# A planner's order searched anew, with later landings of weights and of two batches: packed attention and a squared-ReLU layer on one core

## The chip, the core and the metric

The kernel runs on one core of a Trainium2 chip. The metric is the device time of one execution in microseconds (us). Five engines work in parallel, each through its own queue and in the order in which the program puts instructions into it: TensorE (PE; PEld are its weight loads), VectorE (DVE), ScalarE (ACT), GpSimd (POOL) and SyncE (SP). POOL, SP and ACT also issue the transfers between the device memory and the core's memory. An engine whose first instruction waits holds all that stand behind it.

## What is computed

Eight batches of eight heads, 576 positions, 64 channels a head, and 32 packing queries p per head and batch:

```python
def sm_attn(qq, kk, vv):
    a = softmax(scale * qq @ kk.T)        # per batch and head
    return a @ vv
p_packed = sm_attn(p, k, v)               # 32 x 64 per head
x = sm_attn(q, p_packed, p_packed)        # 576 x 64 per head
h = x.reshape(4608, 512) @ w_in           # 512 x 2048
out = (relu(h) ** 2) @ w_out              # 2048 x 512
```

The second attention has only 32 keys. The kernel never forms x: it multiplies p_packed by w_in first (a matrix M per batch) and the softmax rows by M.

## The kernel before

The work is cut into 1,329 pieces, each with a name, one or two engines that can run it, a cost in us, and the pieces that it needs. For batch b they are:

- `Lk`, `Lv`, `Lq`: loads of k, v and q, issued on POOL, which also converts to bf16 on the way. `LWI.c.i.qd` are the quarters of the four column chunks c of w_in, `LWO.c` the eight chunks of w_out. Each load is two pieces, the issue and the transfer.
- `Tk`, `Tq` (lines 700 and 697 on DVE, 706 on SP for batches 5 to 7): k and q transposed.
- `S1` (PE, line 733 or 749), `MX` (row maximum, DVE, 752), `EX` (exponential, ACT, 760), `E`/`EC` (its transposition, PE 766 and a copy; for batches 5 to 7 `E` is a transposing transfer on SP, line 772), `PV` (PE, 780), `XN`, `XM`, `XC` (normalize, transpose, copy out): the packing attention.
- `M.b.c` (PE, 810): M for chunk c of w_in, copied out by `MC` (ACT line 606 or DVE line 608).
- `S2` (PE, 827 or 837), then the softmax over 32 keys: `SI` (848), `SM` (854), `SU` (858) on DVE, `SE` (exponential, ACT, 861), `SS` (864, 865), `SN` (871), `SO` (875) on DVE. Batch 0 does this in three parts of 128, 192 and 256 positions, named `.0.0`, `.0.1` and `.0.2`.
- `F` (batches 0 and 1, PE line 912) or `F1` (the others, line 884): softmax rows times M into an accumulator pair; `R` (ReLU, ACT 920/894 or DVE 922/896); `Q` or `SQ` (square, ACT 930/902 or DVE 932/904) into the tile gT.
- `F2.t` (PE, 938): 128 rows of the output, sixteen products each, copied out by `FC`. For six groups of four row tiles `GP` (PE, 1005; seven products in two halves of eight instructions) with sums `GS` and `GC` (DVE, 990 and 1025) stand instead. `FZ` (956) is one tile in two halves. `ST` are the stores (line 950).

A planner (`Plan.forward`, from line 73) places these pieces in time when the program is built. It steps through time, and at each moment an engine takes, among the pieces that are ready by the planner's own costs, the one that is lowest in level plus the piece's number in `TABLE['o']`; `TABLE['l']` leans a piece toward DVE or ACT. Only the order of each engine's queue, and the engine, go into the program; on the chip the queues then run as data and buffers allow. A transfer is a piece of a "DMA" engine that runs them one after another; its data counts as there when the piece ends, plus `lag`:

```python
def load(name, us, fn, issue, deps=()):
    old = [issued[-8]] if len(issued) >= 8 else []
    add(f"{name}i", [("POOL", issue, fn)], list(deps) + old, line="load", lag=2.0, level=-200)
    add(name, [("DMA", us, None)], [f"{name}i"], line="dma", lag=0.9, level=-200)
```

Two more rules matter. Where PE changes between kinds of pieces (`mode`: whole-array products 0, `S1` and `S2` 1, `PV` 2, `M` and the later `S1`/`S2` 3) the planner charges `TURN` = 0.111 us. And where PE would idle for 0.7 us or more before the first `F2`, `fills` (line 205) puts products of a zero tile into its queue (line 612), so that PE stays busy; they are in the program for good, and a piece behind them waits for them even when its data is there.

The queues of SP (transposing transfers and stores), ACT (copies, exponentials, ReLU) and DVE are in the planner's hands in the same way; loads are issued by POOL in a fixed list.

Of the kernel before, what the change touches and what calls it, by code (L numbers as in the profile page):

```python
# [14 lines left out]
P = 128  # L15
# [26 lines left out]
class Plan:  # L42
# [185 lines left out]
TABLE = {'o': {'Lk.0.0i': -41.988702, 'Lk.0.1i': 172.502158, 'Lk.0.0': 181.505648, 'LP.0': -6.041854, 'Lk.0.1':  # L228
# [289 lines left out]
def kernel_impl(tc, q, k, v, p, w_in, w_out, out):  # L518
# [23 lines left out]
    with ExitStack() as ctx:  # L542
# [485 lines left out]
        add = plan.add  # L1028
# [36 lines left out]
        for x in ORDER.split():  # L1065
# [29 lines left out]
            elif x[0] == "a":  # L1095
                for i in range(2):
                    for qd in QDS:
                        load(f"LWI.{n}.{i}.{qd}", 0.7 + 0.45 * ((n, i, qd) in ((1, 0, 0), (3, 0, 0), (3, 1, 1))), lambda n=n, i=i, qd=qd: dma_w_in(n, i, qd), 0.6)
# [297 lines left out]
```

## Time and profile before

| | |
|---|---|
| median of 3 runs | 235.95 us (235.69 to 235.96) |
| the profiled execution's own time | 235.75 us |
| its span, first to last instruction | 234.0 us |
| PE / DVE / ACT / POOL busy | 221.4 / 198.1 / 152.0 / 59.9 us |
| PE instructions of line 612 (zero products) | 97, 14.6 us |
| moved by DMA | 34.06 MB |

In a row of a timeline the first two numbers are start and length in us, then follow engine, line, operation, operands and count; in brackets stands the idle time before it and what ended it. A row of the chain of waits has start, length and what the end was waiting for. In a table of stretches each engine's busy time stands in the order of the heading. A row of waits has the total, the number and the longest.

### The profile page before, as it was taken

The numbers are of one execution on the slowest core, as the hardware profiler recorded it, in microseconds if no ns is written. First come the engines' busy times: TensorE is split into PE (matmuls) and PEld (weight loads), VectorE is DVE, ScalarE is ACT, GpSimd is POOL, SyncE is SP. The second block draws the span as 40 slices with busy tenths as digits, with TensorE's granted clock in tenths as the row PEclk, the third lists the DMA queues.
The fourth block names the chain that finished last, engine by engine and source line by source line (L and its number), as shares of the span: only waits on it lengthen the run. The fifth ranks groups of instructions, "written<-read, shape, count | busy, mean of one in ns | idle before, by whom it ended". The sixth has DMA issues, their size and how long they took to land.

```text
span 234.0 us, 6384 instructions
## 1 busy us (share of the span) xinstructions
PE 221.4 (95%) x2621; PEld 159.9 (68%) x2638; DVE 198.1 (85%) x332; ACT 152.0 (65%) x247; POOL 59.9 (26%) x107
## 2 busy tenths in 40 slices
PE   8878899999999999999999999999999999999991
PEld 5655665346554566678768787877777888888781
DVE  3769887799999988999999789999999999877240
ACT  3333897469875799984999846459985998501100
POOL 9777745233343666620000000000000000000000
PEclk9999999999999999999999999999999999999998
DMA  7999999999999999999788689609710023205316
GB/s 235 179 169 175 195 204 204 204 194 250 240 205 241 227 220 177 174 182 125 175 150 135 134 116 191 140 2 204 134 39 8 4 44 73 65 0 112 70 43 181
DMA packets 46716, 34.06 MB, mean 146 GB/s; under 512 B 25376, under 2 KB 38432, under 8 KB 46688
## 3 DMA queue, kind: packets, MB, share of 16 engines
q0 software_dynamic: 19456, 18.03, 48.8%
q1 hardware_dynamic: 26304, 14.98, 29.8%
q10 hardware_dynamic: 928, 0.66, 0.9%
q8 instruction: 20, 0.33, 0.6%
q14 instruction: 8, 0.07, 0.1%
HBM read 37.22 MB, written 9.44 MB: 199 GB/s over the span
## 4 chain that ended last, share of the span: by engine, by line
PE 77%; DMA 14%; DVE 3%; POOL 1%; issue 1%; SPq 1%; ACT 0%; DVEq 0%; POOLq 0%
PE ps L1005 29%; PE ps L884 20%; PE ps L938 13%; DMA kq_b<-in_q_dram 7%; PE ps L912 5%; PE ps L810 3%; DMA w_in_b<-in_moe_w_in_dram 3%; DMA v_b<-in_v_dram 3%; DMA out_dram<-o_sb 2%; PE ps L956 1%; PE ps L780 1%; PE ps L827 1%; SPq L950 1%; PE ps L733 1%; POOL v_b L621 1%
## 5 line engine op out<-in xcount | busy, mean ns | idle before, releaser
L894 ACT ACTIVATE r_b<-ps 128x576 bf16<-128x576 f32 x92 | 52.8, 662 | 8.5 <-PE ps L884 8.3
L884 PE MATMUL ps<-a,M 128*128 128x288 bf16 x384 | 52.5, 286 | 0.2
L884 PEld LDWEIGHTS <-M 128*128 128x128 bf16 x384 | 37.3, 98 | 11.6 <-DVE a L875 0.2
L938 PE MATMUL ps<-w_out_b,gT 128*128 128x512 bf16 x159 | 41.2, 380 | 1.3 <-issue 0.6
L1005 PEld LDWEIGHTS <-gT 128*128 128x128 bf16 x384 | 36.9, 98 | 7.5 <-issue 2.4
L606 ACT CAST M<-ps 128x1024 bf16<-128x1024 f32 (+1 forms) x33 | 29.8, 940 | 10.9 <-PE ps L810 8.7
L904 DVE TENSOR_TENSOR gT<-r_b 128x1152 bf16<-128x1152 bf16 x40 | 29.3, 745 | 4.0 <-ACT r_b L894 3.7
L606 ACT COPY o_sb<-ps 128x512 f32<-128x512 f32 (+1 forms) x21 | 11.9, 575 | 30.5 <-PE ps L1005 16.6
L950 POOL DMA_DIRECT2D out_dram<-o_sb x2 | 1.1, 570 | 119.2 <-DVE o_sb L1025 117.7
L1005 PEld LDWEIGHTS <-gS 128*128 128x128 bf16 x288 | 27.7, 98 | 5.1 <-issue 1.8
L938 PEld LDWEIGHTS <-gT 128*128 128x128 bf16 x176 | 15.8, 98 | 15.3 <-issue 2.5
L1025 DVE TENSOR_TENSOR o_sb<-o_sb,ps 128x512 f32<-128x512 f32 x30 | 20.3, 676 | 6.5 <-PE ps L1005 5.7
L1005 PE MATMUL ps<-wS,gT 128*128 128x256 bf16 x192 | 23.5, 273 | 0.5 <-DVE o_sb L1025 0.5
L1005 PE MATMUL ps<-w_out_b,gT 128*128 128x256 bf16 x192 | 23.8, 273 | 0.0
L1005 PE MATMUL ps<-wS,gS 128*128 128x256 bf16 x192 | 23.5, 273 | 0.0
L920 ACT ACTIVATE r_b<-ps 128x512 bf16<-128x512 f32 (+2 forms) x25 | 15.7, 664 | 7.7 <-PE ps L912 6.4
L912 PE MATMUL ps<-a,M 128*128 128x256 bf16 (+3 forms) x160 | 18.6, 262 | 1.3 <-DVE M L608 0.8
L912 PEld LDWEIGHTS <-M 128*128 128x128 bf16 x160 | 13.8, 98 | 6.4 <-issue 1.1
L760 ACT ACTIVATE e<-ps,n 128x576 bf16<-128x576 f32 x16 | 11.7, 737 | 7.0 <-DVE n L752 6.8
L612 PE MATMUL ps<-o_sb 128*128 128x256 bf16 x97 | 14.6, 311 | 1.1 <-DVE o_sb L615 1.1
L752 DVE TENSOR_REDUCE n<-ps 128x1 f32<-128x576 f32 x16 | 11.6, 750 | 2.0 <-PE ps L733 1.8
L612 PEld LDWEIGHTS <-o_sb 128*128 128x128 bf16 x97 | 10.2, 111 | 4.4 <-DVE o_sb L615 1.1
(77 smaller groups left out, 316.9 us busy)
## 6 DMA issues: line engine op xcount, KB each, us to landing
out_dram<-o_sb SPq DMA_DIRECT2D x65, 128.0 KB, 3.4
kq_b<-in_k_dram POOLq DMA_DIRECT2D x14, 288.0 KB, 10.9
kq_b<-in_q_dram POOLq DMA_DIRECT2D x10, 288.0 KB, 6.9
w_in_b<-in_moe_w_in_dram POOLq DMA_DIRECT2D x16, 128.0 KB, 6.1
w_out_b<-in_moe_w_out_dram POOLq DMA_DIRECT2D x8, 256.0 KB, 9.4
v_b<-in_v_dram POOLq DMA_DIRECT2D x5, 320.0 KB, 11.4
v_b<-in_v_dram POOLq DMA_DIRECT2D x12, 128.0 KB, 7.7
v_b<-in_v_dram POOLq DMA_DIRECT2D x5, 256.0 KB, 9.8
```

The source lines that it names most:

```text
L606: nc.scalar.copy(dst, src)
L612: nc.tensor.matmul(half(7)[:, :2 * P], lhsT=zero[:, :P], rhs=zero, start=True, stop=True)
L752: nc.vector.tensor_reduce(n1[b % 2][:, qd:qd + 1], ps1[b, qd], axis=AX.XY if b in XBAR else AX.X, op=ALU.max, negate=True)
L760: nc.scalar.activation(e_out(qd) if b in XBAR else e1[:, qd, :S], ps1[b, qd], ACT.Exp, bias=n1[b % 2][:, qd:qd + 1], accum_out=d1[b % 2][: ...
L884: nc.tensor.matmul(t[:, c], lhsT=M[b % 2][:, qd, fb * FB:(fb + 1) * FB], rhs=a2[b % 2][:, qd, c * HALF:(c + 1) * HALF], start=(qd == 0), s ...
L894: nc.scalar.activation(dst, src, ACT.Relu)
L904: eng.tensor_tensor(out=dst, in0=r, in1=r, op=ALU.mult)
L912: nc.tensor.matmul(t[:, c, m * w:(m + 1) * w], lhsT=M[b % 2][:, qd, fb * FB:(fb + 1) * FB], rhs=a2[b % 2][:, qd, o:o + w], start=(qd == 0) ...
L920: nc.scalar.activation(dst, ph["h", b, x, j], ACT.Relu)
L938: nc.tensor.matmul(po[t], lhsT=gT[:, fb, n0:n0 + P], rhs=w_out_b[:, fb, :], start=(fb == 0), stop=(fb == NFB - 1))
L1005: nc.tensor.matmul(pz[g, k][:, i], lhsT=a[:, f, i * P:(i + 1) * P], rhs=w[:, f], start=(k not in ON and h == 0 and f == 0 and i == 0), sto ...
L1025: nc.vector.tensor_tensor(out=oC(g, i, j), in0=oC(g, *src), in1=pz[g, z], op=ALU.add)
```

## The change

All numbers of `TABLE` are new. Besides, two lines of the planner's input change:

```diff
-            add(name, [("DMA", us, None)], [f"{name}i"], line="dma", lag=0.9, level=-200)
+            late = 0.8 * (name[:3] == "LWO" or name.split(".")[:2] in (["LWI", "1"], ["LWI", "2"], ["LWI", "3"]) or name[:2] != "LW" and name.split(".")[1] in "12")
+            add(name, [("DMA", us, None)], [f"{name}i"], line="dma", lag=0.9 + late, level=-200)
...
-                        load(f"LWI.{n}.{i}.{qd}", 0.7 + 0.45 * ((n, i, qd) in ((1, 0, 0), (3, 0, 0), (3, 1, 1))), lambda n=n, i=i, qd=qd: dma_w_in(n, i, qd), 0.6)
+                        load(f"LWI.{n}.{i}.{qd}", 0.7 + 0.45 * ((n, i, qd) in ((1, 0, 0), (3, 0, 0))), lambda n=n, i=i, qd=qd: dma_w_in(n, i, qd), 0.6)
...
-TABLE = {'o': {'Lk.0.0i': -41.988702, 'Lk.0.1i': 172.502158, 'Lk.0.0': 181.505648, 'LP.0': -6.041854, 'Lk.0.1':
+TABLE = {'o': {'Lk.0.0i': -36.900503, 'Lk.0.1i': 0.41924, 'Lk.0.0': -16.56608, 'LP.0': 169.009326, 'Lk.0.1':
```

So the planner counts the last three chunks of w_in, all of w_out, and k, v and q of batches 1 and 2 as landing 0.8 us later. No instruction's shape or size changes; what changes is the order. In the two programs, read queue by queue:

- **PE.** Ahead of the last product of `M.0.2` (third chunk of w_in, batch 0) both orders hold the same pieces in the same sequence. Behind it, up to `S1.1`, stood 9 zero products, `F.0.1.0` to `.2`, `M.0.3`, `F.0.2.0` to `.3`, `F.0.1.3`, `F.0.0.2`, `F2.2.0`; now stand `F.0.1.0` to `.2`, `F.0.0.2`, `M.0.3`, `F.0.2.0` to `.5`, 3 zero products, `F.0.2.6`, `F2.3.0`. Zero products are 89 instead of 97. PE changes its kind 65 times behind `M.0.2` instead of 70. In the middle the pieces are dealt anew: between `S1.6` and `PV.6` stand seven halves of `GP`, the four `M.5`, `S2.5` and `XM.5`, where fourteen halves of `GP`, `PV.5` and `S1.7` stood besides the same `M.5`, `S2.5` and `XM.5`; `S1.3` and `S1.4` come earlier. From `GP.1.6` to the end PE's order is the same.
- **ACT and DVE.** Around `M.0.2` ACT had `R.0.0.1`, `MC.0.2.0`, `SE.0.2`, `MC.0.2.1`, `R.0.1.0` to `.2`, `MC.0.3.1`, `R.0.2.0`, `R.0.2.1`; it now has `SE.0.2`, `R.0.0.1`, `Q.0.0.1`, `MC.0.2.1`, `R.0.1.0` to `.2`, `R.0.0.2`, `MC.0.3.1`, `R.0.2.0` to `.2`, `Q.0.2.2`, `R.0.2.3`. `MC.0.2.0` goes to DVE, behind `SS.0.2`; both halves of `MC.0.1` go to ACT. Some 70 pieces in all change their engine.
- **POOL** issues the same loads in the same order; the identity matrix is made two loads earlier. **SP** exchanges neighbours: the two `Tk.5` now stand together ahead of eight stores that stood between them. In the last 20 us ACT, SP and POOL exchange some stores.

577 rows, old and new, of the table TABLE are left out of this document.

## The prediction

> **What bounds the kernel now.** I read the page first, then a table of PE's busy time by stages whose bounds I set at PE's last stall on w_in (24.07) and at the start of `S1.1` (31.90), and that table's row for line 612 alone, the zero products.
>
> ```profile
> span 234.0 us, 6384 instructions
> PE 221.4 (95%) x2621; PEld 159.9 (68%) x2638; DVE 198.1 (85%) x332; ACT 152.0 (65%) x247; POOL 59.9 (26%) x107
> ```
>
> ```profile
> core 0: us, PE busy (x) PEld busy (x) DVE busy (x) ACT busy (x) POOL busy (x), PEclk, DMA share, GB/s
> 0.00:24.07 24.07, 19.53 (x260) 13.14 (x261) 16.11 (x42) 8.04 (x15) 18.48 (x37) 1.00 1.08 189
> 24.07:31.90 7.83, 6.96 (x74) 5.66 (x75) 6.72 (x15) 7.51 (x13) 5.47 (x9) 1.00 1.23 201
> 31.90:96.00 64.10, 62.63 (x804) 35.61 (x816) 57.47 (x106) 50.99 (x88) 29.11 (x51) 1.00 1.21 215
> 96.00:210.00 114.00, 113.74 (x1320) 89.25 (x1323) 108.26 (x158) 83.94 (x130) 5.67 (x11) 1.00 0.57 103
> 210.00:234.00 24.00, 18.59 (x169) 16.28 (x167) 9.57 (x15) 1.54 (x3) 1.14 (x2) 0.96 0.40 99
> ```
>
> ```profile
> 24.07:31.90 7.83, 1.08 (x9) 0.72 (x9) 1.00 1.23 201
> ```
>
> PE is the bound. From 96 to 210 it idles 0.26 us in 114: an order can save there only what the changes between kinds of pieces cost. Time can be had in three places: the start, where PE runs zero products or idles; the stage from 24.07 to 31.90, which loses 0.87 idle + 1.08 of zero products = 1.95 us; and the tail.
>
> **What happens at 24 us.** The timelines of PE, ACT and DVE (a row each; PE's first two are the two parts of `M.0.2`):
>
> ```profile
> 22.52 0.40 PE L810 MATMUL ps<-w_in_b,ppT 64*32 64x512 bf16 x5
> 23.67 0.39 PE L810 MATMUL ps<-w_in_b,ppT 64*32 64x512 bf16 x3 [0.74 <-DMA w_in_b<-in_moe_w_in_dram]
> 24.00 1.16 PE L612 MATMUL ps<-o_sb 128*128 128x256 bf16 x9
> 24.99 2.14 PE L912 MATMUL ps<-a,M 128*128 128x192 bf16 x24
> 27.67 1.06 PE L912 MATMUL ps<-a,M 128*128 128x256 bf16 x8 [0.20 <-DVE a L875]
> 29.18 2.29 PE L912 MATMUL ps<-a,M 128*128 128x256 bf16 x24 [0.45 <-DVE M L608]
> 31.90 0.71 PE L733 MATMUL ps<-kT,pT 32*32 32x512 bf16 x32 [0.22 <-DVE r_b L922]
> ```
>
> ```profile
> 24.10 0.59 ACT L606 CAST M<-ps 128x512 bf16<-128x512 f32 x1 [0.87 <-PE ps L810]
> 24.58 0.63 ACT L861 ACTIVATE e<-s 128x512 bf16<-128x512 f32 x1
> 25.11 0.58 ACT L606 CAST M<-ps 128x512 bf16<-128x512 f32 x1
> 25.85 2.23 ACT L920 ACTIVATE r_b<-ps 128x768 bf16<-128x768 f32 x3 [0.16 <-PE ps L912]
> 27.97 0.59 ACT L606 CAST M<-ps 128x512 bf16<-128x512 f32 x1
> 28.43 1.12 ACT L920 ACTIVATE r_b<-ps 128x512 bf16<-128x512 f32 x2
> 29.58 0.63 ACT L930 ACTIVATE gT<-r_b 128x512 bf16<-128x512 bf16 x1
> ```
>
> ```profile
> 21.23 0.68 DVE L608 CAST M<-ps 128x512 bf16<-128x512 f32 x1
> 22.56 0.63 DVE L858 TENSOR_TENSOR s<-s,m 128x512 f32<-128x512 f32 x1
> 25.25 0.69 DVE L864 TENSOR_REDUCE t<-e 128x16 f32<-128x512 bf16 x1 [0.91 <-ACT e L861]
> 27.17 0.45 DVE L875 STREAM_TRANSPOSE a<-n 128x256 f32<-128x256 f32 x1
> ```
>
> The third chunk of w_in lands late, and PE stands 0.74 us in the middle of `M.0.2`. The dearer part is indirect. On ACT the copy `MC.0.2.0` stands ahead of `SE.0.2`, the exponential of the third softmax part. That one's input was ready at 22.56 + 0.63 = 23.19, but ACT was held by the copy until 24.10 and began it at 24.58. So DVE idled 0.91 and handed over the part at 27.62, and PE began `F.0.2.0` at 27.67. Nine zero products, put in for a gap that the planner saw here, meanwhile ran behind a stall that had already used it up.
>
> **The change part by part.**
>
> *Up to 24.07: nothing.* PE's pieces up to `M.0.2` are the same, the loads go out in the same order, and the last three products of `M.0.2` wait for the landing at 23.6. Zero products ahead of it go from 88 to 86, and `F.0.0.1` now waits for a copy that ACT makes behind another, some 0.4 us later; all of that lies under the landing. If that cover is gone (the chunk lands earlier here), it costs up to those 0.4 us; I take 0.
>
> *24.07 to `S1.1`: -0.75.* `SE.0.2` now stands ahead of both copies, and of the copy of the second chunk (21.23, 0.68) DVE is rid, so the exponential starts near 22.7. What binds then is ACT's queue. I add it up from starts in the rows: exponential 0.53 (24.58 to 25.11), ReLU of 512 columns 0.5 (half of 1.12, less the overlap), square 0.63 and 0.15 for its own input, copy 0.46 (27.97 to 28.43), ReLU of 768 columns 2.12 / 3 = 0.71 (25.85 to 27.97). In the new order: `SE.0.2` to 23.2, `R.0.0.1` to 23.7, `Q.0.0.1` to 24.5, `MC.0.2.1` to 25.0, three ReLU to 27.1, `R.0.0.2` to 27.6, `MC.0.3.1` to 28.1, `R.0.2.0` to `.2` to 29.6, `Q.0.2.2` to 30.4, `R.0.2.3` to 30.9. That frees the accumulators for `F.0.2.6` at 31.0; with its four products (0.45) and one of `F2.3` and a change of kind (0.3) PE is at `S1.1` near 31.75, 0.15 earlier than 31.90. And it has done more: 60 instructions of line 912 instead of 56, twelve more of 256 columns (2.29 / 24 = 0.095 each at least, 0.11 by the spacing below) and eight fewer of 192 (2.14 / 24 = 0.09), 1.31 - 0.71 = 0.6 us. Together -0.75. Bounds: 0 if the softmax part is still last, because DVE now has `MC.0.2.0` (0.68) between `SS.0.2` and `SN.0.2`; -1.95 if nothing at all is lost there. The sum lies nearer to the rows of ACT, so I take -0.75.
>
> *Behind it: -0.55 for five changes of kind fewer.* The chain of waits, in which each row ends where the next begins:
>
> ```profile
> 94.39 0.87 PE ps L1005 x8
> 95.26 0.34 PE ps L810 x8
> 95.60 0.98 PE ps L1005 x8
> ```
>
> Eight products of line 1005 take 0.98 right behind `M` and 0.87 ahead of it: a change costs 0.11. 70 - 65 = 5 changes, 0.55 us, on the engine that bounds. The Trainium skill says in "TensorEngine Tiling (Array Packing)", Key Properties, that changing the tiling mode drains TensorE, and in "TensorE: Matmul & The Clock Gate", Single matmul latency, gives 398 cycles at 2.4 GHz beside the columns; taking all of that as the drain would make 0.166 us a change and 0.83 in all, an estimate. The trace has 0.11, and that is what the sum uses.
>
> *Behind it: other waits, 0.* From 31.90 to 96 PE idles 1.47 us in many small pieces, part of it at these changes. PE's waits of that stage name w_out nowhere, so a lead of 0.75 us should find it landed. I take the same idle time after; bounds -0.9 (most of the rest goes) and +1.0 (as much again, from new neighbours on DVE, busy 57.47 of 64.10).
>
> *Tail: 0.* PE waits once; the chain of waits, PE's timeline and the list of transfers have:
>
> ```profile
> 213.58 4.05 DMA out_dram<-o_sb
> ```
>
> ```profile
> 218.49 1.03 PE L1005 MATMUL ps<-wS,gT 128*128 128x256 bf16 x8 [0.54 <-DVE o_sb L1025]
> ```
>
> ```profile
> out_dram<-o_sb SPq DMA_DIRECT2D x65, 128.0 KB, 3.4
> ```
>
> A sum on DVE needs the output buffer that the last of four stores frees, whose transfer took 4.05 us; it starts as late behind `GP.6.6` in the new order (two stores have changed places), and PE's 0.54 stays.
>
> **Sum.** 235.75 for the profiled execution (span 234.0 and 1.75 around it) - 0.75 - 0.55 = 234.45. The median of the runs is 0.2 above that execution, so I forecast **234.6 us**. From the bounds (-1.95 -0.55 -0.9 and 0 -0.55 +1.0) the forecast alone could lie anywhere from 232.5 to 236.4; both ends need every term at its extreme.
>
> **Rivals.**
>
> *Only the changes of kind.* The softmax of the third part stays last and -0.75 falls away: 235.95 - 0.55 = 235.4. For it: `MC.0.2.0` on DVE. Against: the exponential gains 1.9 us (24.58 to 22.7), of which that copy takes 0.68 back.
>
> *The order does nothing on the chip.* What the planner shifts, other queues give back; 235.95.
>
> *Slower: `PV.6` comes too early for its transposition.* `E.6` is a transfer on SP, behind two transpositions of k:
>
> ```profile
> 134.38 0.45 PE L749 MATMUL ps<-kT,pX 64*32 64x256 bf16 x32
> 149.60 0.49 PE L780 MATMUL ps<-v_b,e 128*32 128x64 bf16 x40
> ```
>
> ```profile
> 134.95 3.68 SPq L706 DMA_TRANSPOSE kT<-kq_b x2
> 138.79 1.37 SPq L772 DMA_TRANSPOSE e<-e x1
> ```
>
> ```profile
> e<-e SPq DMA_TRANSPOSE x3, 3.5
> DMA to landing us min/median/max: 3.4/4.0/10.4
> ```
>
> Before, `PV.6` came 15.2 us behind `S1.6`, and its operand was there 138.79 + 3.5 - 134.38 = 7.9 us behind it. In the new order PE has 0.4 (`S1.6`) + 7 x 0.87 (`GP`) + 1.9 (`M.5`, `S2.5`, `XM.5` and their changes) = 8.4 us of work in between, so 0.5 us of cover are left of 7.3. A transposition that takes 3.5 + 0.5 + x holds PE for x; slower by the measurable amount begins at x = 0.47 + 1.35 = 1.8 (the bound below, and the gain to be used up), a transfer of 5.8 us. Such exist (the transpositions of k reach 10.4, but that one ran beside loads, which are over by then). With 6.5 us x is 2.5: 237.1.
>
> *More.* The store in the tail takes 3.4, the median of its kind, and the 0.54 us go too, with some of the idle time to 96: 233.8.
>
> *The clock.* Fewer zero products keep PE less busy. The granted clock is 1.00 in all stages up to 210 and 0.73 where products have ended:
>
> ```profile
> 230.00:234.00 4.00, 0.00 (x0) 0.00 (x0) 0.00 (x0) 0.00 (x0) 0.00 (x0) 0.73 0.49 153
> ```
>
> A PE that stood as long as there, about 4 us, and ran on at that clock for as long would lose 4 / 0.73 - 4 = 1.5 us: 236.1. Zero products still stand in the start's long waits, 86 of 88. By the Trainium skill, "TensorE: Matmul & The Clock Gate", What's actually happening, an idle window of about 3.4 us halves the clock and a busy one restores it; the trace agrees as far as its last row shows.
>
> **How the numbers follow.** Chances: forecast 0.55, only the changes of kind 0.14, nothing 0.09, `PV.6` 0.10, more 0.09, clock 0.03. A measurement tells 0.2% from no change, 0.47 us: faster is below 235.48. Forecast, "more" and two thirds of "only the changes" are faster, 0.73; the other third, "nothing" and the clock are the same, 0.17; `PV.6` is slower, 0.10. The range, 233.7 to 235.9, takes in forecast, "more" and "only the changes".
>
> **What would show it.** Right: `SE.0.2` on ACT starts ahead of 23.2; `S1.1` starts at 31.7 to 31.8; no nine zero products behind `M.0.2`, which still ends near 24.07; from 96 to 210 as little idle time as now; 0.5 us idle ahead of `GP.3.7`. Wrong: `M.0.2` ending elsewhere than 24.07, PE idle ahead of `PV.6` or `PV.7`, more than 2.5 us idle between 31.9 and 96, or a granted clock below 1.00 ahead of 225.

## The result, and the profile after

The changed kernel takes **233.60 us** (median of 8 runs, 233.22 to 235.06) against 235.28 us for the kernel before on the same chip (8 runs, 234.81 to 235.96): a ratio of **0.9934**, 95% interval 0.9909 to 0.9959, 1.55 us less. The same instructions, timed once more later, gave 0.9932 (0.9905 to 0.9958). The forecast was 234.6 us, 1.35 less than the 235.95 us of the runs of before known then. The profiled execution took 233.42 us, 2.33 less than that of before.

The page of the changed kernel begins with its span and the busy times:

```profile
span 231.7 us, 6374 instructions
PE 220.0 (95%) x2613; PEld 160.0 (69%) x2630; DVE 199.4 (86%) x336; ACT 148.4 (64%) x243; POOL 60.5 (26%) x108
```

The table of stretches with the same bounds:

```profile
0.00:24.07 24.07, 19.88 (x264) 13.73 (x265) 16.25 (x42) 9.20 (x17) 19.79 (x38) 1.00 1.07 189
24.07:31.90 7.83, 7.07 (x85) 5.34 (x90) 7.49 (x17) 7.67 (x15) 3.91 (x8) 1.00 1.19 195
31.90:96.00 64.10, 62.61 (x819) 36.67 (x817) 59.66 (x109) 45.23 (x81) 29.63 (x52) 1.00 1.21 215
96.00:210.00 114.00, 113.79 (x1308) 89.61 (x1313) 107.70 (x156) 84.98 (x130) 5.49 (x10) 1.00 0.62 104
210.00:231.70 21.70, 16.63 (x153) 14.66 (x150) 8.34 (x13) 1.33 (x3) 1.67 (x3) 0.93 0.44 110
```

From 31.9 to 210 PE idles as before (1.49 + 0.21 us, before 1.47 + 0.26), and the clock is 1.00 up to 210. `S1.6` starts at 133.77 and `PV.6` at 142.17, 8.4 us behind it as the prediction worked out, and PE does not idle ahead of it. PE's timeline (source lines are 3 higher in this kernel: 615, 813, 915 and 830 are 612, 810, 912 and 827 of before):

```profile
17.18 0.58 PE L830 MATMUL ps<-qT,pq 32*32 32x192 bf16 x28 [0.36 <-DVE qT L700]
22.43 0.46 PE L813 MATMUL ps<-w_in_b,ppT 64*32 64x512 bf16 x8
23.53 2.69 PE L915 MATMUL ps<-a,M 128*128 128x192 bf16 x32 [0.64 <-DVE a L878]
26.19 0.41 PE L813 MATMUL ps<-w_in_b,ppT 64*32 64x512 bf16 x8
26.89 1.08 PE L915 MATMUL ps<-a,M 128*128 128x256 bf16 x8 [0.29 <-ACT r_b L923]
28.26 1.91 PE L915 MATMUL ps<-a,M 128*128 128x256 bf16 x16 [0.28 <-DVE M L611]
30.00 0.49 PE L615 MATMUL ps<-o_sb 128*128 128x256 bf16 x3
31.43 0.70 PE L736 MATMUL ps<-kT,pT 32*32 32x512 bf16 x32
210.75 1.91 PE L1008 MATMUL ps<-w_out_b,gT 128*128 128x256 bf16 x16
215.99 1.04 PE L1008 MATMUL ps<-wS,gT 128*128 128x256 bf16 x8
```

`M.0.2` runs without a stall and has ended at 22.89, not at 24.07; the third chunk of w_in landed at 22.45 here. What PE then waits for is the *second* softmax part: `F.0.1.0` starts at 23.53, behind its transposition on DVE (line 878). `S1.1` starts at 31.43. In the tail the 0.54 us ahead of `GP.3.7` (215.99) are gone. ACT's and DVE's timelines:

```profile
22.48 0.63 ACT L864 ACTIVATE e<-s 128x512 bf16<-128x512 f32 x1 [0.60 <-DVE s L861]
```

```profile
23.10 0.38 DVE L878 STREAM_TRANSPOSE a<-n 128x192 f32<-128x192 f32 x1
26.25 0.45 DVE L878 STREAM_TRANSPOSE a<-n 128x256 f32<-128x256 f32 x1 [0.22 <-PE ps L915]
```

Three rows of before are needed beside these, PE's start of the last 28 products of line 827 in the start (`S2.0.1` and `S2.0.2`), its start of `GP.0.7`, and the second softmax part's transposition on DVE:

```profile
17.31 0.58 PE L827 MATMUL ps<-qT,pq 32*32 32x192 bf16 x28 [0.72 <-DVE qT L697]
212.55 1.91 PE L1005 MATMUL ps<-w_out_b,gT 128*128 128x256 bf16 x16
```

```profile
23.97 0.37 DVE L875 STREAM_TRANSPOSE a<-n 128x192 f32<-128x192 f32 x1
```

Those 28 products wait for the second half of q, whose landing differs from one execution to the next. So the start is best counted from them; I call that point Q. The two profiled executions then divide like this (the 0.6 us of work is the prediction's estimate):

| us | before | after | difference |
|---|---|---|---|
| first instruction to Q | 17.31 | 17.18 | -0.13 |
| Q to `S1.1` | 14.59 | 14.25 | -0.34, with 0.6 us more work done |
| `S1.1` to `GP.0.7` | 180.65 | 179.32 | -1.33, with those 0.6 us less to do |
| `GP.0.7` to `GP.3.7` | 5.94 | 5.24 | -0.70 |
| `GP.3.7` to the last instruction | 15.51 | 15.71 | +0.20 |

At equal work the start gave 0.94 us, the middle 0.73, the tail 0.70. How much of this belongs to the order, and how much to these two executions, is what the experiments ask.

### The profile page after: what moved, and what is told of

The parts are those of the page before. It is cut to its first block, busy times and chain, and to the rows that moved or that the text cites. A ratio compares the mean times of both kernels' runs of the same rounds, so it can differ in the third digit from the quotient of the medians.

```text
span 231.7 us, 6374 instructions
## 1 busy us (share of the span) xinstructions
PE 220.0 (95%) x2613; PEld 160.0 (69%) x2630; DVE 199.4 (86%) x336; ACT 148.4 (64%) x243; POOL 60.5 (26%) x108
## 4 chain that ended last, share of the span: by engine, by line
PE 83%; DVE 6%; DMA 5%; POOL 1%; issue 1%; ACT 1%; DVEq 0%; ACTq 0%; POOLq 0%
PE ps L1008 32%; PE ps L887 21%; PE ps L941 15%; PE ps L915 4%; PE ps L813 3%; DMA v_b<-in_v_dram 3%; DMA kq_b<-in_q_dram 2%; PE ps L959 2%; DVE gT L935 1%; PE ps L783 1%; PE ps L830 1%; PE ps L736 1%; PE ps L769 1%; POOL v_b L624 1%; DVE qT L700 1%
## 5 line engine op out<-in xcount | busy, mean ns | idle before, releaser
L897 ACT ACTIVATE r_b<-ps 128x576 bf16<-128x576 f32 x86 | 50.4, 663 | 10.1 <-PE ps L887 9.7
L609 ACT CAST M<-ps 128x1024 bf16<-128x1024 f32 (+1 forms) x30 | 26.9, 933 | 12.4 <-PE ps L813 12.3
L609 ACT COPY o_sb<-ps 128x512 f32<-128x512 f32 (+1 forms) x23 | 12.9, 568 | 32.2 <-PE ps L1008 18.4
L953 POOL DMA_DIRECT2D out_dram<-o_sb x3 | 1.7, 556 | 108.8 <-ACT o_sb L609 103.6
L907 DVE TENSOR_TENSOR gT<-r_b 128x1152 bf16<-128x1152 bf16 x37 | 27.1, 746 | 1.6 <-ACT r_b L897 1.6
L1008 PE MATMUL ps<-wS,gT 128*128 128x256 bf16 x192 | 24.0, 273 | 0.0
L923 ACT ACTIVATE r_b<-ps 128x512 bf16<-128x512 f32 (+2 forms) x30 | 17.8, 659 | 4.8 <-PE ps L915 4.7
L915 PE MATMUL ps<-a,M 128*128 128x256 bf16 (+3 forms) x160 | 18.3, 262 | 2.2 <-DVE a L878 1.0
L615 PE MATMUL ps<-o_sb 128*128 128x256 bf16 x89 | 13.9, 319 | 1.1 <-DVE o_sb L618 1.1
L864 ACT ACTIVATE e<-s 128x1152 bf16<-128x1152 f32 (+4 forms) x11 | 10.0, 912 | 6.2 <-DVE s L861 6.1
```

The costliest lines, as they stand in the source:

```text
L609: nc.scalar.copy(dst, src)
L615: nc.tensor.matmul(half(7)[:, :2 * P], lhsT=zero[:, :P], rhs=zero, start=True, stop=True)
L897: nc.scalar.activation(dst, src, ACT.Relu)
L907: eng.tensor_tensor(out=dst, in0=r, in1=r, op=ALU.mult)
L915: nc.tensor.matmul(t[:, c, m * w:(m + 1) * w], lhsT=M[b % 2][:, qd, fb * FB:(fb + 1) * FB], rhs=a2[b % 2][:, qd, o:o + w], start=(qd == 0) ...
L923: nc.scalar.activation(dst, ph["h", b, x, j], ACT.Relu)
```

## The experiments

In each, the order of every engine is written out as a list instead of being searched, so that only the named pieces move; line numbers are those of the kernel before. Ratios are to the kernel before on the same chip.

**1. The exponential first.** ACT's list of the kernel before:

```diff
 R.0.0.1
-MC.0.2.0
 SE.0.2
+MC.0.2.0
 MC.0.2.1
```

> The kernel before with one change: on ACT `SE.0.2` stands ahead of `MC.0.2.0`. The nine zero products behind `M.0.2` stay. Theory A (the late exponential was the dear thing between 24.07 and 31.90, and it binds together with the zero products): the exponential starts at 23.2, its transposition on DVE (line 875) near 26.0 instead of 27.17, but PE still runs the nine zero products and 24 products of line 912 up to 27.1, so that only the 0.20 us ahead of `F.0.2.0` and a part of the 0.45 us ahead of 29.18 can go: 0 to -0.4 us, a ratio of 0.998 to 1.000, `S1.1` at 31.5 to 31.9. Rival B (the exponential alone was the dear thing): -0.75 us, ratio 0.997, `S1.1` near 31.2. Rival C (ACT's queue binds anyway): `S1.1` stays at 31.90, ratio 1.000.

Ratio 1.0001 (0.9979 to 1.0023). The exponential did start earlier, 5.91 us behind Q instead of 7.27; ACT's and PE's timelines:

```profile
23.53 0.63 ACT L861 ACTIVATE e<-s 128x512 bf16<-128x512 f32 x1
```

```profile
27.77 1.05 PE L912 MATMUL ps<-a,M 128*128 128x256 bf16 x8 [0.20 <-DVE a L875]
32.00 0.70 PE L733 MATMUL ps<-kT,pT 32*32 32x512 bf16 x32 [0.22 <-DVE r_b L922]
```

The same 0.20 and 0.22 us of idle time stand ahead of `F.0.2.0` and `S1.1` as before: neither became free by the earlier exponential. Q was at 17.62.

**2. No nine zero products.** In the list of zero products of the kernel before:

```diff
-ahead of F.0.1.0: 9
```

> The kernel before without the nine zero products behind `M.0.2`, and nothing else. Theory A: `F.0.1.0` starts at 24.1 instead of 24.99, but `F.0.2.0` still waits for the third softmax part, at 27.6; PE idles there for what it saved, `S1.1` stays at 31.8 to 31.9, ratio 0.999 to 1.000. Rival D (the zero products alone were the dear thing): -0.9 us at `S1.1`, ratio 0.996.

Ratio 1.0001 (0.9978 to 1.0024), as Theory A had it, but the idle time stands at another place:

```profile
25.56 2.15 PE L912 MATMUL ps<-a,M 128*128 128x192 bf16 x24 [1.46 <-DVE a L875]
32.49 0.42 PE L733 MATMUL ps<-kT,pT 32*32 32x512 bf16 x8 [0.22 <-DVE r_b L922]
```

PE waits 1.46 us for a transposition on DVE ahead of `F.0.1.0`: for the second softmax part, not for the third. DVE had not idled; the square `Q.0.0.1` and the copy `MC.0.1.0` (at 22.40) stood ahead of that transposition:

```profile
24.80 0.42 DVE L932 TENSOR_TENSOR gT<-r_b 128x512 bf16<-128x512 bf16 x1
25.14 0.37 DVE L875 STREAM_TRANSPOSE a<-n 128x192 f32<-128x192 f32 x1
```

With Q at 18.48, `F.0.1.0` is 7.08 behind it and `S1.1` 14.01.

**3. Both.** The two diffs together.

> The kernel before with both changes of the two runs ahead of this one: `SE.0.2` ahead of `MC.0.2.0` on ACT, and no nine zero products. Theory A: now PE can use the early softmax part; `F.0.2.0` starts near 26.5, `S1.1` at 30.9 to 31.3, -0.6 to -1.0 us, ratio 0.9958 to 0.9975, more than the sum of the two runs ahead of it. Rival C (ACT's queue, with its copies and ReLU, binds from 24 on): `S1.1` not ahead of 31.6, ratio 0.999.

Ratio 1.0009 (0.9985 to 1.0032). Theory A is wrong: PE's timeline has the same wait, and `S1.1` again 14.01 us behind Q.

```profile
17.66 0.58 PE L827 MATMUL ps<-qT,pq 32*32 32x192 bf16 x28 [1.02 <-DVE qT L697]
24.75 2.15 PE L912 MATMUL ps<-a,M 128*128 128x192 bf16 x24 [0.99 <-DVE a L875]
```

The times of runs 2 and 3 hold one thing more. Every execution has a granted clock, the mean over its whole span; in the profiles without a fall ahead of the tail it is 0.994 to 1.000. Of the 12 executions each, 3 of run 2 and 5 of run 3 had 0.989 to 0.991 and took 236.26 and 235.92 us on average; the others took 234.86 and 234.82. Of runs 1 and 4, which keep the nine zero products, none in 24 had less than 0.994, and of before beside them 4 in 35 (0.989 to 0.993). So on this chip PE seems to lose its clock more often without the nine. None of these executions was profiled, and run 6 below, without the nine too, has none. The other executions of runs 2 and 3 are 0.2 us faster than the other 31 of before (235.02), too little to tell.

**4. Old start, new rest.**

```diff
-order = before
+order = [x for x in before if x starts ahead of S2.1.0] + [x of after that are left]
```

> The order of the kernel before for all that starts ahead of `S2.1.0` (PE at about 44 us), and the changed kernel's order for all that is left; so the start is the old one, and the five changes of kind are saved. Prediction's split (-0.75 in the start, -0.55 by five changes of kind, tail unchanged): -0.55 us, ratio 0.9977; `S1.1` at 31.9 as before. Rival E (most of the gain comes from behind the start, from other waits and the tail): -1.2 us or more, ratio 0.995 or less, and no idle time ahead of `GP.3.7`. Rival F (all of the gain is in the start, changes of kind cost nothing): ratio 1.000. `SE.0.2`'s delay and the landing of the third w_in chunk near 23.6 should be as before.

Ratio 0.9981 (0.9961 to 1.0000). With Q at 17.42, `S1.1` came 14.01 us behind it and `GP.0.7` 194.56; in runs 2 and 3 that is 194.65 and 194.70, in the changed kernel 193.57. So the ratio fits the prediction's split (0.9977), but counted from Q only 0.1 of 1.1 us came with the rest of the order. The seam would account for 0.53 more: PE's two rows at it,

```profile
41.29 0.91 PE L810 MATMUL ps<-w_in_b,ppT 64*32 64x512 bf16 x16
43.10 0.99 PE L827 MATMUL ps<-qT,pq 32*32 32x256 bf16 x32
```

take 0.63 and 0.74 us in the changed kernel. This searched order could not be cut in two there without such a loss.

The runs so far, counted from Q, and those that follow (from the starts in PE's timeline; runs 10 to 12 load w_in in another order and are told there):

| run | Q at | Q to `S1.1` | Q to `GP.0.7` | `GP.0.7` to `GP.3.7` |
|---|---|---|---|---|
| before | 17.31 | 14.59 | 195.24 | 5.94 |
| 1 exponential first | 17.62 | 14.38 | 195.06 | 5.64 |
| 2 no nine | 18.48 | 14.01 | 194.65 | 5.24 |
| 3 both | 17.66 | 14.01 | 194.70 | 5.24 |
| 4 old start | 17.42 | 14.01 | 194.56 | 5.31 |
| 5 more changes | 19.05 | 14.52 | 196.11 | 5.25 |
| 6 DVE rid | 17.41 | 14.18 | 194.82 | 5.24 |
| 7 exponential last | 17.99 | 15.74 | 195.05 | 5.24 |
| 8 back on DVE | 17.44 | 16.75 | 196.20 | 5.24 |
| after | 17.18 | 14.25 | 193.57 | 5.24 |
| 9 after, again | 17.79 | 14.26 | 193.58 | 5.24 |

The old order takes 14.01 us to `S1.1` and 194.6 to 194.7 to `GP.0.7` unless w_in is late: in "before" PE stood 0.74 us for it, in run 1 0.53, and lost 0.58 and 0.37 at `S1.1`. What it lost them by is told behind runs 10 to 12.

**5. Twenty more changes of kind.** Ten times in PE's list of the changed kernel, like this:

```diff
-GP.1.2.0, M.3.1, M.3.2
+M.3.1, GP.1.2.0, M.3.2
```

> The changed kernel with ten pairs of neighbouring pieces of one kind (two of `M`, of `S2`, or `M` and `S2`) parted by a piece of 128 by 128 products taken from just behind or ahead of them: 95 changes of kind instead of 75, with the same instructions and the same work. At 0.11 us each, as the prediction has it: +2.2 us, a ratio to the kernel before of 0.9934 + 0.0094 = 1.003. If a change costs nothing: 0.9934. If it costs 0.166 us: +3.3 us, 1.0075. In the trace the stretch from `S1.1` to `GP.0.7` took 179.32 us in the changed kernel; it should take 181.5, 179.3 or 182.6.

Ratio 1.0037 (1.0004 to 1.0069). From `S1.1` to `GP.0.7` PE took 215.16 - 33.57 = 181.59 us, 2.27 more than in the changed kernel:

```profile
33.57 0.70 PE L733 MATMUL ps<-kT,pT 32*32 32x512 bf16 x32
```

```profile
215.16 1.91 PE L1005 MATMUL ps<-w_out_b,gT 128*128 128x256 bf16 x16
```

That is 0.1135 us a change: the price of the prediction, 0.11, stands, and 0.166 falls. (Q came at 19.05 and w_in late, so its time as a whole says less; the stretch behind `S1.1` does not move with that, 179.31 to 179.45 us in the changed kernel and runs 7 to 9.)

**6. DVE rid of two pieces.** Lists of the kernel before, the nine zero products taken out too:

```diff
 ACT: R.0.0.0
+SE.0.1, MC.0.1.0
 MC.0.1.1
-SE.0.1
+SE.0.2
 R.0.0.1
+Q.0.0.1
-MC.0.2.0, SE.0.2
 MC.0.2.1
 DVE: Q.0.0.0
-MC.0.1.0
 SS.0.1, SU.0.2, SN.0.1
-Q.0.0.1
 SO.0.1, SS.0.2
+MC.0.2.0
 SN.0.2
```

> The kernel before without the nine zero products and with the changed kernel's places for four pieces: `MC.0.1.0` and `Q.0.0.1` on ACT instead of DVE, `SE.0.2` ahead of `MC.0.2.0`, and `MC.0.2.0` on DVE ahead of `SN.0.2`. PE's order is that of before. Times are counted from the start of the last products of line 827 in the start, which wait for q to land. The runs so far give for `S1.1` 14.01 us behind that point, with the zero products or without, and with `SE.0.2` first or not. Theory G (what held PE was the second softmax part: its transposition on DVE, line 875, 6.66 us behind that point, stood behind `MC.0.1.0` and `Q.0.0.1`): that transposition comes near 5.9, `F.0.1.0` near 6.3 instead of 7.0, and `S1.1` near 13.3; -0.6 to -0.8 us, ratio near 0.997. Rival C (ACT's queue binds, and with two pieces more it binds harder): `S1.1` at 14.0 or later, ratio 1.000 or more.

The transposition came 5.92 us behind Q (23.33) and `F.0.1.0` 6.47, nearly as Theory G had it; `S1.1` did not follow: 14.18. PE's timeline shows where it stayed:

```profile
23.88 0.82 PE L912 MATMUL ps<-a,M 128*128 128x192 bf16 x8 [0.81 <-ACT r_b L920]
25.16 0.90 PE L912 MATMUL ps<-a,M 128*128 128x192 bf16 x9 [0.46 <-DVE M L608]
26.52 0.74 PE L912 MATMUL ps<-a,M 128*128 128x192 bf16 x7 [0.45 <-DVE a L875]
```

Three short waits, for a ReLU, a copy and a transposition, took the place of one. The copy is `MC.0.2.0`, which this run moves to DVE, and `SE.0.1` changes its place too, so the run does not show what the two pieces alone are worth. The ratio was 0.9968 (0.9945 to 0.9990), better than this trace explains: its `GP.0.7` is 0.1 to 0.3 us later than in the old order with w_in in time. About half of it is the clock: none of its ten executions (234.64 to 235.13 us) had less than 0.994, but of the executions of before beside them 7 of 30 had 0.989 to 0.993 and took 236.48 us on average, the other 23 235.25 (one more, of 238.14 us, is left out). Against those 23 run 6 is 0.40 us faster. Why that much stays open.

**7. The exponential last, in the new order.** ACT's list of the changed kernel:

```diff
 MC.0.1.1
-SE.0.2
 R.0.0.1, Q.0.0.1, MC.0.2.1
+SE.0.2
 R.0.1.0
```

> The changed kernel with one piece moved back: on ACT `SE.0.2` stands behind `MC.0.2.1`, so that it begins near 24.5 as in the kernel before, and the rest is the changed kernel. Theory A in its weak form (in the new order, where the second softmax part comes early, the place of the exponential does decide): `F.0.2.0` 1 to 1.5 us later, `S1.1` 1.0 to 1.5 us later than the changed kernel's 14.14 us behind the start of the last products of line 827; ratio to the kernel before 0.998 to 1.000. Rival H (the exponential's place is worth nothing in this order either): ratio 0.9934.

Ratio 0.9988 (0.9969 to 1.0007), `S1.1` 15.74 behind Q: 1.49 us later than the changed kernel's 14.25 (the 14.14 in the expectation counts from the first product of `S2.0.2`, 0.11 later). PE waits in the middle of `F.0.1`:

```profile
27.23 1.28 PE L912 MATMUL ps<-a,M 128*128 128x192 bf16 x16 [1.40 <-DVE M L608]
```

for `MC.0.2.0`, which on DVE now stands behind `SS.0.2`, and that waits for the exponential:

```profile
25.65 0.69 DVE L864 TENSOR_REDUCE t<-e 128x16 f32<-128x512 bf16 x1 [1.36 <-ACT e L861]
```

In the old order, where that copy ran on ACT, the exponential's place was worth nothing; in the new one it is worth 1.5 us.

**8. Two pieces back on DVE.** Lists of the changed kernel:

```diff
 DVE: Q.0.0.0
+MC.0.1.0
 SS.0.1, SU.0.2, SN.0.1
+Q.0.0.1
 SO.0.1
 ACT: SE.0.1
-MC.0.1.0
 MC.0.1.1, SE.0.2, R.0.0.1
-Q.0.0.1
 MC.0.2.1
```

> The changed kernel with `MC.0.1.0` and `Q.0.0.1` put back on DVE where the kernel before has them, and nothing else. Theory G: the transposition of the second softmax part (DVE, line 878 in the changed kernel) goes from 5.8 to 6.6 us behind the start of the last products of line 827, and `F.0.1.0` and `S1.1` come 0.7 to 1.1 us later; ratio to the kernel before 0.9965 to 0.998. Rival C (ACT's queue binds, and is relieved): no loss or a gain, ratio 0.993 or less.

Ratio 1.0040 (1.0011 to 1.0069): in this order the two pieces are worth 2.5 us, more than the whole change. PE's timeline and two stretches (in a row of stretches PE's busy time stands behind the length, and the granted clock is the third number from the end):

```profile
25.25 3.72 PE L912 MATMUL ps<-a,M 128*128 128x192 bf16 x32 [2.20 <-DVE a L875]
```

```profile
23.00:25.00 2.00, 0.06 (x8) 0.08 (x1) 1.36 (x5) 1.59 (x3) 1.29 (x3) 1.00 1.22 201
27.00:30.00 3.00, 3.00 (x26) 2.14 (x25) 1.72 (x5) 2.41 (x4) 1.28 (x3) 0.50 1.23 203
```

The wait for the second softmax part grew from 0.64 to 2.20 us, since the square on DVE now waited for a ReLU that ACT makes behind `SE.0.2`:

```profile
24.49 0.42 DVE L932 TENSOR_TENSOR gT<-r_b 128x512 bf16<-128x512 bf16 x1 [0.64 <-ACT r_b L920]
```

And after that wait the clock was 0.50 for more than three us: 32 products took 3.72 us, in the changed kernel 2.69. `F.0.1.0` starts 7.81 us behind Q instead of 6.35, and from there to `S1.1` it takes 8.94 instead of 7.90. So 1.46 us are the wait and about 1.0 the clock. The ten executions agree: seven had a clock of 0.982 to 0.993 and took 236.77 us on average, the other three 235.11.

**9. The changed kernel again.** The same instructions.

> The changed kernel's instructions once more, nothing altered. Counted from the start of the last products of line 827, which wait for q to land, the runs so far reach `GP.0.7` 194.56 to 194.70 us later in the old order where no other transfer was late (three profiles), and 193.57 us later in the changed kernel. Theory I (the order itself is worth that difference, 1.1 us, and what the first comparison showed beyond it, 1.55 us, was the luck of late transfers): ratio near 0.9953, and the profile again reaches `S1.1` at 14.2 to 14.3 and `GP.0.7` at 193.5 to 193.6 unless w_in is late. Rival J (the order is worth the full 1.55 us because it also makes late transfers rarer): ratio 0.993 to 0.994, with q landing and w_in's third chunk landing no later than in the first profile (16.4 and 22.5).

Ratio 0.9932 (0.9905 to 0.9958). The trace repeats: 14.26 and 193.58 us behind Q. And w_in was late this time:

```profile
17.79 0.58 PE L827 MATMUL ps<-qT,pq 32*32 32x192 bf16 x28 [1.37 <-DVE qT L697]
23.68 0.39 PE L810 MATMUL ps<-w_in_b,ppT 64*32 64x512 bf16 x3 [0.24 <-DMA w_in_b<-in_moe_w_in_dram]
24.14 2.68 PE L912 MATMUL ps<-a,M 128*128 128x192 bf16 x32
32.05 0.70 PE L733 MATMUL ps<-kT,pT 32*32 32x512 bf16 x32
```

The third chunk came as late as in the kernel before (23.67 there), and it cost nothing: `F.0.1.0` starts at 24.14 as it would have anyway, 6.35 behind Q. In run 5, where the chunk came 6.3 us behind Q (25.38 - 19.05), it cost 0.27. The ratio leaves both open: its interval holds Theory I's 0.9953 and Rival J's 0.993 to 0.994. The places in the trace are Theory I's, and, as far as two profiles tell, the landings speak against Rival J (q 16.99 and w_in 23.64 here, 16.38 and 22.45 in the first profile): late transfers did come again, and this order lost nothing by them here.

**10 to 12. A late chunk, with and without the nine.** The kernel before, in the list of loads:

```diff
-a1 a2 a3 k1
+a1 a3 a2 k1
```

(a2 and a3 are the third and fourth chunk), in run 11 and 12 without the nine zero products as well.

> The kernel before with one change: the fourth chunk of w_in is loaded ahead of the third, so that the third, which `M.0.2` needs, lands about 2 us later (near 26 instead of 23.6). The orders of PE, DVE and ACT are those of before, and the nine zero products stand behind `M.0.2`. Theory K (the zero products cost time just when w_in is late: a landing far behind uses up the gap that they were put in for): `M.0.2` ends near 26.3, the nine run behind it, and `F.0.1.0` starts 0.9 us behind the end of `M.0.2` as in the first profile (24.07 to 24.99). `S1.1` comes 1.5 to 2.5 us later than the 14.01 us behind the start of the last products of line 827. Whatever the theory, the run is slower than before by 1.5 to 2.5 us; what tells is the comparison with the next run.

> The same as the run ahead of this one, without the nine zero products. Theory K: `F.0.1.0` starts at most 0.2 us behind the end of `M.0.2`, and the time from that end to `S1.1` is 0.7 to 1.0 us shorter than in the run ahead. Rival L (what comes behind binds, as it did where w_in was in time, so that the zero products are covered here too): from the end of `M.0.2` to `S1.1` the two runs differ by less than 0.2 us.

> The instructions of the run on the late third chunk without the nine zero products, once more. There the last quarter of the chunk came 0.84 us later than in the run with them (26.24 against 25.40), PE had idled 2.35 us in four pieces, and the granted clock fell to 0.50 from 24.8 to 31.5, so that the two could not be compared. If the quarter lands by about 25.6 and the clock stays at 1.00 up to 34: Theory K has 6.9 to 7.1 us from the end of `M.0.2` to `S1.1` (7.84 with the nine), Rival L 7.7 to 7.9. If the clock falls again with a landing that early, the nine zero products are what keeps it up there (Rival M), and the run is again slower than the one with them.

Ratios 1.0122 (1.0034 to 1.0209), 1.0149 (1.0033 to 1.0265), 1.0111 (1.0081 to 1.0140). PE behind `M.0.2` in runs 10, 11 and 12:

```profile
25.77 1.16 PE L612 MATMUL ps<-o_sb 128*128 128x256 bf16 x9
26.76 2.14 PE L912 MATMUL ps<-a,M 128*128 128x192 bf16 x24
```

```profile
26.28 0.61 PE L810 MATMUL ps<-w_in_b,ppT 64*32 64x512 bf16 x3 [1.11 <-DMA w_in_b<-in_moe_w_in_dram]
26.83 4.02 PE L912 MATMUL ps<-a,M 128*128 128x192 bf16 x24
```

```profile
25.36 0.61 PE L810 MATMUL ps<-w_in_b,ppT 64*32 64x512 bf16 x3 [0.56 <-DMA w_in_b<-in_moe_w_in_dram]
25.90 3.38 PE L912 MATMUL ps<-a,M 128*128 128x192 bf16 x24
```

The first half of Theory K holds: without the nine, `F.0.1.0` follows `M.0.2` at once (run 12 25.90 against run 10 26.76, with the quarter landing at 25.32 and 25.40). But in runs 11 and 12 the clock fell to 0.50, and the 24 products took 4.02 and 3.38 us instead of 2.14. That is Rival M's sign, but not its cause: by stretches of one us the fall began near 24.7 and 25.1, ahead of the place where the nine would stand, and of run 10's two executions, with the nine, one had 0.989 too. No run has the late chunk without the nine in a profile at full clock; one execution of run 12 had a clock of 1.000 and took 237.25 us, against 236.92 for the profiled one of run 10, and when its chunk landed is not known. So what the nine cost when w_in is late was not measured.

It can be worked out from the rows. In the old order `S1.1` comes 6.91 to 6.93 us behind `F.0.1.0` in before and runs 1 to 4, and 6.91 in run 10; in run 12 it is 8.15, and 6.91 without the 1.24 us that the 24 products lost. So `F.0.1.0` decides. With w_in in time it starts 7.08 us behind Q (runs 2 to 4), behind the second softmax part. In before it starts 7.68 and in run 1 7.46 behind Q, right behind the nine, while `M.0.2` had ended 6.75 and 6.53 behind Q. If nothing else then holds PE, both could have started at 7.08 without the nine: the late chunk alone would have cost nothing, and the nine behind it cost 0.60 and 0.38, close to the 0.58 and 0.37 that `S1.1` lost.

## Why the prediction was right, and where it was wrong

The size was nearly right, 1.35 forecast and 1.55 measured, and faster it was: at the measured ratio the 235.95 us of the forecast become 234.4, inside its range. But one of the signs that the prediction named for being wrong came true: `M.0.2` ended at 22.89, not at 24.07. By its own steps:

**"Up to 24.07: nothing" failed.** It took `M.0.2`'s end at 24.07, and the landing behind it, for a fact of the program. The same list of loads in the same order brought the last quarter of the third chunk at 21.95 to 25.38 in the profiles of before, after and runs 1 to 9. A stall on a load seen in one profile need not come in the next. Without the stall `S1.1` of the old order would have stood at 17.31 + 14.01 = 31.32, not at 31.90, so the stage was measured against a place that this one execution had.

**"24.07 to `S1.1`: -0.75" has the wrong cause.** It named the copy ahead of `SE.0.2` on ACT. The exponential did move as forecast (22.48, forecast ahead of 23.2), but runs 1 to 3 show that in the old order neither it nor the nine zero products, nor both, gave a gain that can be measured: the wait of 1.46 us in run 2 is for the second softmax part, which stood on DVE behind `MC.0.1.0` and `Q.0.0.1`. In the profile of before that wait could not be seen, since the nine zero products and the stall on w_in lay over it. The reading that the nine ran behind a stall that had used up their gap fits that profile (0.60 us by the working above), but only while w_in is late. "What binds then is ACT's queue" was half right: in the new order PE waits between `M.0.2` and `S1.1` for DVE (0.64 and 0.28 us) and for ACT (0.29 and 0.19). Taking the two pieces off DVE, with three others moved, did not bring `S1.1` forward in the old order of PE (run 6); in the new order, the exponential put back costs 1.3 us of the whole time and the two pieces put back 2.5 (runs 7 and 8), 1.0 of it by the clock. The gain of the start belongs to the placement as a whole: Q to `S1.1` goes from 14.01 to 14.25 with 0.6 us more work done, -0.36 us where -0.75 was forecast. The other 0.58 of the 0.94 us is the late chunk with the nine behind it in the one profile of before; the new order, which has no zero products there, lost 0 and 0.27 in the two profiles with a late chunk (runs 9 and 5).

**"-0.55 for five changes of kind" holds** as far as run 5 shows, which prices a change at 0.1135 us, five at 0.57. Run 4, which has the five changes less, shows 0.10 in the trace, 0.63 with what its seam took. By the Trainium skill, "TensorEngine Tiling (Array Packing)", Key Properties, a change of tiling mode drains TensorE; the trace agrees that a change costs time. The estimate of 0.166 us a change, worked out from the Trainium skill, "TensorE: Matmul & The Clock Gate", Single matmul latency, is not borne out: 0.1135 was measured.

**"Other waits: 0"** came to -0.16, what is left of the middle's 0.73 us when 0.57 are taken off, inside its bounds. No run shows it by itself.

**"Tail: 0" failed for this pair of executions.** The 0.54 us ahead of `GP.3.7` went (`GP.0.7` to `GP.3.7` 5.94 to 5.24). What decides is how long the last of four stores takes. In run 1, with the old tail, the chain of waits has it again, shorter:

```profile
213.71 3.75 DMA out_dram<-o_sb
```

Of eight profiles with the old order of stores two had a loss above 0.05 us (0.70 and 0.40), of six with the new one one (0.07). That does not tell the two orders apart; the rival "more" had named the mechanism and its size, 0.54 us.

**Sum.** By order alone, from runs 2, 3 and 9: 194.65 or 194.70 to 193.57, 1.1 us = 0.36 + 0.57 + 0.16. What was measured lies 0.45 above that, inside its interval of 0.6; but the second comparison gave 1.6, so chance alone explains it poorly. Lateness accounts for some of it: over before and runs 1 to 4 w_in, with the nine behind it, cost 0.19 us on average, in the three profiles of the new start (after, 5 and 9) 0.09; and the tail's loss was 0.14 on average with the old stores and 0.01 with the new. The granted clock does not explain it in run 9's comparison, where all 17 executions of both kernels had 0.994 or more. The rest is not settled. That the forecast of 1.35 came so near is in part luck: the start, with the wrong cause, gave 0.36 by the order instead of 0.75, and lateness, the tail and the rest made up for it; only the changes of kind were right in cause and size.

**Rivals.** "Only the changes of kind" (0.55 us) and "nothing" lie outside the measured interval of 1.0 to 2.1 us; "`PV.6` too early" fell, since PE did not idle ahead of `PV.6`. "More" (2.15 us) lies at the edge of the interval. "The clock" did not happen in the changed kernel, whose executions all had 0.994 or more, but runs 8, 11 and 12 show its mechanism and price, 1.0 to 1.9 us over the products of line 912, after waits shorter than the 4 us that it assumed.

## What to carry to other kernels

Count a stage from the event that starts it, here a landing: behind Q the two profiled executions of the changed kernel agree within 0.01 us in 193, while their whole times differ by 0.6 us and the runs of one comparison by up to 1.8, so a change of 1.1 us in 235 can be taken apart from single profiles. An idle gap names what ended it last, not what binds: fill products and a chance stall can cover the true wait, and only removing the named one shows it. Pieces of a searched order are not worth what they seem one by one: two of its moves, alone and together, gave nothing that can be measured in the old order, and each of the two undone in the new one cost about as much as the whole change, or more. And zero products that look useless may be guarding the clock: on one chip 8 of 24 executions had a lowered one without the nine and 4 of 59 with them, though no trace shows it at work and on another chip 7 of 30 had it with them.

## What the runs showed of the hardware

- A PE that stood 2.20 us and had been busy 0.06 us in two (run 8) was granted half its clock afterwards, by stretches of one us from about 26.6 to 30.0, so the clock fell about 1.4 us after PE had gone on working; waits of 1.46 us (run 2) and 1.40 us (run 7) had no such effect in the profiled executions. The Trainium skill, "TensorE: Matmul & The Clock Gate", What's actually happening, speaks of an idle window of about 3.4 us; here a gap of 2.2 us was enough, and the measurement decides. In run 11, with short work between waits, the half clock lasted from about 24.7 to 31.5:

```profile
26.00:31.00 5.00, 4.72 (x35) 3.70 (x34) 1.83 (x5) 3.23 (x6) 2.05 (x4) 0.50 1.22 200
```

  It began after waits of 0.69, 0.33 and 0.22 us, while run 10 with 0.77, 0.31 and 0.23 us at the same place kept 1.00. So the length of the waits alone does not decide.

- With the loads issued in one order, the last transfer of q's second half, issued at 11.0 to 11.4 us, landed between 16.4 and 18.3 us in the profiles of before, after and runs 1 to 9, and the last quarter of the third chunk of w_in between 22.0 and 25.4. The second spread holds some of the first: POOL waits for q before it issues that quarter (at 16.7 to 18.6 us), and from its issue to its landing it took 4.9 to 6.8 us. In before:

```profile
16.81 0.58 POOL L688 DMA_DIRECT2D w_in_b<-in_moe_w_in_dram  x1 [1.02 <-DMA kq_b<-in_q_dram]
```
